# A fused attention and Mish layer on one core: packing the normalised output of four heads into dense 128-row tiles

## The chip, the cores and the metric

The kernel runs on one core of one Trainium2 chip. The time is the device time of one execution in microseconds (us). Five engines work side by side, each through its own instructions in order: PE (TensorE, matrix products), ACT (ScalarE, here above all exponentials), DVE (VectorE), POOL (GpSimd) and SP (SyncE, which here issues nearly all DMAs). A *profiled execution* is one execution taken by the hardware profiler; its *span* goes from the first to the last instruction.

## The reference

```python
def _A_ref(x, wqkv, wo):                      # x: 1 x 2048 x 640, bf16
    H = 32; Dh = 20
    q, k, v = (x @ wqkv) ...                  # each 32 heads x 2048 x 20
    p = softmax(q @ k.T * Dh ** -0.5)         # per head, 2048 x 2048
    return (p @ v) ... @ wo                   # heads side by side, then 640 x 640

def _B_ref(x, w1, b1, w2):                    # 640 -> 1536 -> 640
    h = x @ w1 + b1
    return (h * tanh(softplus(h))) @ w2       # Mish

g = sigmoid((x * gate_w).sum(-1))
return g * _A_ref(x, wqkv, wo) + (1 - g) * _B_ref(x, w1, b1, w2)
```

The bulk of the work is the softmax: 32 heads of 2048 x 2048 exponentials.

## The kernel before

**Heads and groups.** The 2048 query rows are cut into four chunks `c` of 512, the 32 heads into eight groups `g` of four heads. A head has only 20 channels, and the four heads of a group sit at steps of 32 rows of the 128 partitions, so that PE can work on four heads side by side in four strips of 32 rows. KT and QT hold keys and queries in this form. A *unit* is the score tile of one head for 128 keys and 512 queries; the kernel has 4 x 8 x 16 x 4 = 2048 of them. The work goes through groups (c, g): first chunks 0 and 1 in turn for each g, then chunk 2, then chunk 3, whose last group is cut into two halves of 256 queries (`CUTS`).

**Steps.** Three units make a *step* (`SLOT`), 683 in all. In each step PE computes three score tiles into PSUM (`score_mms`, line 1291), ACT exponentiates them (`emit_e`, line 1312) into ETS, and PE multiplies the exponentials of four heads by V (`pv`, line 1616), summing over the keys in one PSUM bank per group. A column of ones in V (row 0 of each head's 32 rows) gives the softmax's denominator. Two steps' scores are in PSUM at a time.

**Tiles given to DVE.** In many steps one of the three units goes to DVE instead (`choose`, `emit_x`, line 1358). DVE writes a scaled score as int16, whose bits read as fp16 are a rough exponential. Four such units make a *batch*; two shifted versions of it (`close`, line 1396, functions `below` and `above`) are added to the sum, so a batch is multiplied by V three times (named Y, U, E). A batch lives in buffers (pads) of 4 x 512 columns that are lent by other tensors while these are not in use: parts of PADS, W2R, REG, HB, KT, QT (`("q", n)`) and OTN (`("o", n)`). The follow-up instructions wait in queues (`soon`, of which there are `LANES`), out of which `work` fills DVE's time. The functions `patient` and `settle` may move some multiplications to POOL.

**The planner.** The order of every instruction on every engine is fixed ahead of the run, by a plan that is made in Python: `Plan.add` keeps an estimated time per engine, and the loop over the steps (lines 2002 to 2076) puts background tasks on PE where its estimate leaves room (`pick`, `put`), each with a due step. `choose` decides whether a step gives a unit to DVE, from DVE's estimated backlog, corrected by a hand-set list `NUDGE` (one value per eight steps), and from the tasks that are late (`room`, `behind`, `lag`). `fill_up` adds dummy products (`spin`, line 1983) where PE would stream less than the share `STREAM` or `SPUN` of a window of some 3.6 us.

**After a group.** `group_done` copies the sums out of PSUM to OUNG (line 1749), sends the denominators through a DMA to POOL (line 1767), which inverts them (line 1771), and through SUMS back to all rows (lines 1774 and 1780, four DMAs). Then one multiplication (`times`, line 1709) on DVE or POOL writes the normalised group to its place given by `otn`: OTN for chunks 0 and 1, QT for chunks 2 and 3. The place keeps the heads' steps of 32 rows: 80 of 128 rows hold data. The last groups of chunk 3 (from `DIRECT`) are inverted on DVE without DMAs.

**Output projection.** `p_task` multiplies one tile of 128 queries by one half (320 columns) of the output weights WOG, which lie in WOQ in the same form with zero rows in between (`load_wo`): a *half tile*, one product per group, eight in all, through `p_mm` and the helper `tall` (line 557). `tall` may issue a product as four of 32 rows. For chunk 3, `part_task` does the six groups that are done early and stores to PART; the last two groups (`late`) are added at the end (lines 2084 to 2110). `mix` (line 1124) applies the gate and adds the dense layer's part.

**Dense layer.** `load_w1` (line 976) brings w1 in pieces of 256 columns through two buffers, `h_task` computes h, `mish` the activation (line 1053 on ACT, 1077 and 1080 on DVE), `b_task` the product by w2. These run from some 210 us on, interleaved with the output projection.

**Queues.** SP issues its DMAs in the plan's order; each waits on SP for what it depends on. K and Q for groups 2 to 7 go through DRAM: packed products are stored (line 706, `shelve`) and fetched into the 32-row form (line 730, `fetch`). The packed K products are staged in OTN, in columns 6 and 7 of its eight (line 695).

Of the kernel before, what the change touches and what calls it, by code (L numbers as in the profile page):

```python
# [14 lines left out]
ALU = mybir.AluOpType  # L15
AX = mybir.AxisListType

P = 128
S = 2048
D = 640  # L20
NF = 1536
H = 32
DH = 20
NG = 8
# [15 lines left out]
OWE = -0.5  # L40
# [14 lines left out]
STREAM = 0.46  # L55
SPUN = 0.5
# [10 lines left out]
CALM_END = 20  # L67
# [3 lines left out]
LANES = 1  # L71
# [8 lines left out]
GIVE_BACK = 25  # L80
# [8 lines left out]
BEYOND = 0.4  # L89
SOONER = 3  # L90
# [11 lines left out]
PATIENCE = 5  # L102
# [4 lines left out]
EAGER = 65  # L107
LOAD = 0.85
MISH = 3.5
GROUP = 2.25  # L110
LAST = 0
END = 45
SHIFT = 0.4
LAG = 45
SPARE = 5
WINDOW = 3.6
# [14 lines left out]
PART_DUE = 15  # L131
LAST_DUE = 23
# [20 lines left out]
LEAD = 10  # L153
NUDGE = [1.5, -3.5, -4.2, -3.7, 0.8, 2.3, -2.2, 0, -5.3, 1.5, 0.7, 2.3, -1.5, 0, -3.7, -1.5, 6, 0.0, 2.3, 0, 0, -3.7, 0.8, -0.7, 1.5, 3.7, -3, 1.5, 0.8, 3.0, 1.5, 6, -0.7, -0.7, 5, 2.2, 0.0, 1.4, 2.2, 0.8, 1.5, 6, 0.0, 2.2, -0.7, 3.5, -3.0, 0.0, -3.7, -1.5, 0.6, -2.3, 1.5, -0.7, -0.7, 0.7, 5, -0.7, 0, 2.9, 0.7, 0.7, 6, 0, 0, 0.7, -0.7, -0.7, 5, -1.5, 1.5, 0.7, 1.5, -3.8, -2.2, -3.0, 1.5, 0, 6, -3.8, 1.5, 0.7, -3, 1.5, -3, 2.8, 6]
# [116 lines left out]
def bass_gated_mix__softmax_full_mha__dense_activation_mish__prompt_kernel(  # L271
# [97 lines left out]
    def pad_at(home):  # L369

        kind, n = home
        if kind == "p":
            return PADS[:, n, :].rearrange("p (a b t) -> p a b t", a=2, t=CW)
        if kind == "h":
            return HB[:, 1, 0:8, :].rearrange("p f t -> p (f t)").rearrange("p (a b t) -> p a b t", a=2, t=CW)
        if kind == "k":
            return KT[:, n, :].rearrange("p (a b t) -> p a b t", a=2, t=CW)
        if kind == "q":
            return QT[:, 2 * n:2 * n + 2, 0:2 * CW].rearrange("p a (b t) -> p a b t", t=CW)
        if kind == "o":  # L380
            return OTN[:, n // 2, n % 2 * 4:n % 2 * 4 + 4, :].rearrange("p (a b) t -> p a b t", a=2)
        return AREAS[n][1].rearrange("p (a b t) -> p a b t", a=2, t=CW)
# [37 lines left out]
    def attention(pl, fast):  # L420
# [178 lines left out]
        if fast:  # L599
# [102 lines left out]
            def shelve(k, name, c, rows, src, ev, n, i=0):  # L702
# [436 lines left out]
        late = every[len(early):]  # L1139
        last_t = [t for t in range(4) if not fast or t * P >= CUTS[-1][0]]  # L1140
# [15 lines left out]
        def p_task(c, t, half, due, rest=False):  # L1156

            tb = c * 4 + t
            some = late if rest else every
            needed = [g for g in some if g < NG - 1]  # L1160
            needed.append(next((k[1] for k, (at, w) in cut.items() if k[0] == c and at <= t * P < at + w), NG - 1))

            def ready():
# [4 lines left out]
                if fast and len(wog_ready) < 2 * HG + 1 or rest and (t, half) not in part_done:  # L1168
                    return None
                return [otn_done[(c, g)] for g in needed] + wog_ready  # L1170

            def finish(bank, last):
                otn_read[c % 2].append(last)
                if fast and c < 2 and len(otn_read[c]) == 8:
                    gained.extend(("o", 2 * c + i) for i in range(2))
                    pad_free.update({at: [last] for at in gained[-2:]})
# [21 lines left out]
        def part_task(t, half, due):  # L1198
# [14 lines left out]
            return Task([p_mm(c, t, half, g, early) for g in early], HALF * COL, finish, due, ready)  # L1213
# [33 lines left out]
        def emit_s(s):  # L1247
# [23 lines left out]
            if fast and order:  # L1271
                here = order[0][:2]
                for n in range(NG // 2):
# [4 lines left out]
                    if place[here] >= place[(2, 2 * n)]:  # L1278
                        given_back.add(at)
# [409 lines left out]
        spread_last = []  # L1689
        end_done = []  # L1690

        def group_done(c, g, step, last):
# [7 lines left out]

            def reads():
                if fast:
                    assert c != 2 or not pad_busy(("q", g // 2))
                    return [low_last[0], *lent(("q", g // 2), c == 2)] if c >= 2 else [zeros, *turned, *(k_moved if g >= 6 else ())]
                assert c < 2 or g > 0 or len(otn_read[c % 2]) == 8
                return otn_read[c % 2]

            def times(src, deps, eng="dve"):
                oung_free[0] = bc_read[0] = otn_done[(c, g)] = pl.add(eng, lambda e: e.tensor_tensor(
                    otn(c, g, fast), src, BC, ALU.mult), [*deps, *reads()], cost=WIDE if eng == "dve" else ASIDE, kind="L")  # L1710
                if g == NG - 1:
                    otn_read[c % 2] = []
# [543 lines left out]
```

## Time and profile before

| | |
|---|---|
| median of three runs | 767.94 us (767.77 to 768.16) |
| profiled execution, its own time | 767.94 us |
| its span | 766.1 us |
| first exponential tiles on ACT / last instruction | 9.06 us / 766.1 us |
| DMA traffic | 46.73 MB, mean 61 GB/s |

How to read the rows that follow in the prediction: a group row gives line, engine, operation, out<-in with the names of the program's tensors, the shape, the number of instructions (x), then `|` the busy time in us and the mean duration of one in ns, then `|` the engine's idle time just ahead of these instructions and what ended it. A row of the chain of waits gives start, length, engine, what was written, and line, in us. A row of the timeline gives start, length, engine, line, operation and shapes. Busy time is the union of an engine's instructions; a row that has a line number is a place in the kernel above.

### The profile page before, as it was taken

How to read it: one execution, taken by the hardware profiler on the slowest of the kernel's cores; microseconds unless marked ns; L12 is line 12 of the kernel's file. 1: busy time of each engine (PE TensorE's matmuls, PEld its weight loads, DVE VectorE, ACT ScalarE, POOL GpSimd, SP SyncE). 2: the span in 40 equal slices, each digit the busy share in tenths (PEclk: the TensorE clock that was granted, in tenths of full speed). 3: DMA queues.
4: the chain of work that ended last, by engine and by line, in shares of the span. 5: the costliest groups of instructions: out<-in, count | busy, mean ns of one | idle time of the engine just before them, and what ended most of it. 6: DMA issues, size and time to landing. Idle time of an engine off the chain costs nothing.

```text
span 766.1 us, 19028 instructions
## 1 busy us (share of the span) xinstructions
PE 731.2 (95%) x7922; PEld 272.4 (36%) x7922; DVE 697.0 (91%) x1325; ACT 751.1 (98%) x714; POOL 121.4 (16%) x60
## 2 busy tenths in 40 slices
PE   8999999899999999999999899999999999999996
PEld 4333334233333333222334433333333333433333
DVE  4789798899898999998999999999999999998895
ACT  6999999999999999999999999999999999999996
POOL 8111121011112021111011102121202111022000
PEclk9999999999999999999999999999999999999999
DMA  7411310221123312140113411022212213000001
GB/s 157 132 56 51 91 50 25 59 66 50 40 74 124 94 59 65 50 132 30 37 46 100 115 36 45 26 57 78 67 28 68 84 38 87 16 25 20 15 7 39
DMA packets 76586, 46.73 MB, mean 61 GB/s; under 512 B 23204, under 2 KB 72732, under 8 KB 76444
## 3 DMA queue, kind: packets, MB, share of 16 engines
q1 hardware_dynamic: 76380, 45.41, 21.3%
q8 instruction: 66, 1.08, 0.6%
q14 instruction: 28, 0.23, 0.1%
q0 software_dynamic: 112, 0.01, 0.1%
HBM read 35.74 MB, written 7.51 MB: 56 GB/s over the span
## 4 chain that ended last, share of the span: by engine, by line
ACT 83%; PE 15%; DVE 2%; issue 0%
ACT ETS L1312 80%; PE PS L1291 4%; PE PS L1616 4%; PE PS L557 3%; ACT REG L1053 2%; PE PS L1983 1%; ACT W2R L1053 0%; PE PS L635 0%; PE PS L936 0%; PE PS L829 0%; PE PS L866 0%; PE PS L764 0%; DVE WOQ L747 0%; DVE HB L2108 0%; PE PS L816 0%
## 5 line engine op out<-in xcount | busy, mean ns | idle before, releaser
L1312 ACT ACTIVATE ETS<-PS 128x1024 bf16<-128x1024 f32 (+1 forms) x683 | 731.1, 1279 | 3.1 <-PE PS L1291 2.3
L1291 PE MATMUL PS<-QT,KT 32*128 32x512 bf16 (+1 forms) x2112 | 270.8, 378 | 18.9 <-ACT ETS L1312 13.7
L1616 PE MATMUL PS<-ETS,V_all 128*21 128x512 bf16 (+1 forms) x1643 | 176.3, 375 | 0.0
L1771 POOL TENSOR_TENSOR RR<-RR,NEG 128x16 f32<-128x16 f32 x29 | 89.2, 3076 | 490.3 <-DMA RR<-OUNG 490.3
L1291 PEld LDWEIGHTS PS<-QT,KT 32*128 32x128 bf16 x2112 | 67.4, 91 | 231.0 <-ACT ETS L1312 179.7
L557 PE MATMUL PS<-XB,REG 128*32 128x256 bf16 (+3 forms) x716 | 82.1, 292 | 3.8 <-DVE HB L1030 1.6
L1358 DVE TENSOR_SCALAR QT<-PS 128x512 int16<-128x512 f32 x115 | 77.9, 686 | 6.4 <-PE PS L1291 5.8
L1358 DVE TENSOR_SCALAR PADS<-PS 128x512 int16<-128x512 f32 x106 | 71.7, 685 | 5.3 <-PE PS L1291 4.4
L557 PE MATMUL PS<-W2R,HB 128*128 128x320 bf16 (+1 forms) x600 | 73.0, 301 | 1.6 <-DVE XB L1102 0.6
L1358 DVE TENSOR_SCALAR OTN<-PS 128x512 int16<-128x512 f32 x79 | 53.7, 684 | 4.0 <-PE PS L1291 3.4
L557 PEld LDWEIGHTS PS<-XB,REG 128*128 128x128 bf16 (+1 forms) x716 | 38.1, 96 | 38.2 <-issue 28.9
L1616 PEld LDWEIGHTS PS<-ETS,V_all 128*21 128x21 bf16 x1643 | 41.3, 90 | 28.1 <-issue 23.1
L1080 DVE TENSOR_TENSOR U<-U 128x1024 f16<-128x1024 f16 x72 | 49.2, 683 | 0.2
L557 PEld LDWEIGHTS PS<-W2R,HB 128*128 128x128 bf16 (+1 forms) x600 | 33.2, 97 | 31.7 <-issue 16.0
L1358 DVE TENSOR_SCALAR REG<-PS 128x512 int16<-128x512 f32 x59 | 40.0, 687 | 3.7 <-PE PS L1291 3.2
L1030 DVE TENSOR_TENSOR HB<-PS,B1T 128x512 bf16<-128x512 f32 x48 | 32.8, 683 | 3.7 <-PE PS L557 3.3
L1358 DVE TENSOR_SCALAR KT<-PS 128x512 int16<-128x512 f32 x39 | 26.7, 686 | 5.7 <-PE PS L1291 5.6
L1077 DVE TENSOR_SCALAR U<-U 128x1024 f16<-128x1024 f16 x72 | 30.3, 420 | 0.5
L1396 DVE TENSOR_SCALAR QT<-QT 128x2048 int16<-128x2048 int16 (+2 forms) x62 | 29.2, 492 | 1.2 <-PE PS L1616 1.1
L557 PE MATMUL PS<-XB,WOQ 128*32 128x512 bf16 (+1 forms) x164 | 28.6, 382 | 0.8 <-DVE WOQ L775 0.4
L1358 DVE TENSOR_SCALAR W2R<-PS 128x512 int16<-128x512 f32 x35 | 23.7, 686 | 2.4 <-PE PS L1291 2.0
L557 PE MATMUL PS<-WOQ,QT 128*128 128x320 bf16 (+1 forms) x188 | 24.2, 301 | 1.6 <-DVE HB L1124 0.7
(173 smaller groups left out, 797.6 us busy)
## 6 DMA issues: line engine op xcount, KB each, us to landing
REG<-in_B_w_dram SPq DMA_DIRECT2D x36, 320.0 KB, 3.2
BCT<-SUMS SPq DMA_DIRECT2D x116, 64.0 KB, 2.1
W2R<-in_B_w_dram SPq DMA_DIRECT2D x12, 320.0 KB, 3.3
KT<-KS SPq DMA_DIRECT2D x28, 128.0 KB
QT<-QS SPq DMA_DIRECT2D x112, 20.0 KB
QS<-WOQ SPq DMA_DIRECT2D x16, 128.0 KB, 1.7
KS<-OTN SPq DMA_DIRECT2D x16, 128.0 KB, 1.7
W2R<-in_B_w_dram SPq DMA_DIRECT2D x1, 1920.0 KB, 8.2
```

The costliest lines, as they stand in the source:

```text
L557: op = e.matmul(PS[at, bank, cols], w[:, at], x, start=start, stop=stop, **({"tile_position": (0, i * rows)} if parts > 1 else {}))
L1030: ev = dve(lambda e: e.tensor_tensor(hb, PS[:, bank, :].rearrange("p (i t) -> p i t", i=2), bias, ALU.add), [last, b_load, *guarded, *b_re ...
L1053: ex = pl.add("act", lambda e: e.activation(U, h, AF.Tanh, scale=0.5, bias=-MISH_AT), [ev, u_free[0]], cost=0.95)
L1077: return lambda e: e.tensor_scalar(dst, src, *ops)
L1080: return lambda e: e.tensor_tensor(dst, one, two, ALU.mult)
L1291: op = pl.add("pe", lambda e, i=i, g=real(g), tile=tile, j=j, cols=cols, c=c, of_q=of_q: e.matmul(scores(s)[:, i, cols], KT[32 * j:32 * j ...
L1312: e_op[s] = pl.add("act", lambda e: e.activation(EXPS[:, at:at + n, :], scores(s)[:, 0:n, :], AF.Exp, scale=SCALE, bias=LIFT if fast else ...
L1358: ev = dve_by(lambda e: e.tensor_scalar(block(batch["y"], n, I16), scores(s)[:, 2, :], SCALE * ULPS, BIAS, ALU.mult, ALU.add), [s_op[s], * ...
L1396: op = pl.add("dve", lambda e, sp=sp: e.tensor_scalar(some_of(home, sp, I16), some_of(y, sp, I16), by, None, ALU.add), deps, cost=each, ki ...
L1616: lasts[n] = pl.add("pe", lambda e, v=v, j=j, src=src[:, cols], of_q=of_q, count=count: e.matmul(PS[32 * j:32 * j + EW, bank, of_q], v, sr ...
L1771: r = (pl.add("pool", lambda e: e.tensor_tensor(RR[:, :], RR[:, :], NEG[:, :].to_broadcast([P, 16]), ALU.pow), [got, m_neg], cost=INVERT) ...
L1983: pl.add("pe", lambda e: e.matmul(PS[:, bank, :], k[:, 0:P], k, start=True, stop=True), [free], cost=PASS, kind="S")
```

## The change

The normalised output of chunks 0 to 2, and of groups 0 to 5 of chunk 3, is no longer left in the 32-row form. `times` writes it to one of two staging places (column 5 of OTN's two halves); then DMAs on SP (`move`) copy each head's 20 rows, cut at multiples of 128, to dense tiles of 128 rows: channel `r` of the 640 goes to row `r % 128` of tile `r // 128`, five tiles per chunk, in OTN for chunks 0 and 1 and in QT for 2 and 3 (`packed`). The output weights are loaded dense as well (WOP, three DMAs), and in 32-row form for the last two groups alone (WOL, `spread_out`). A half tile then takes five products over 128 rows; `part_task` takes four (480 rows: three full tiles and one of 96); the late two groups remain as they were.

With it go three changes of buffers: OTN lends columns 0 to 3 of each half once its chunk is projected, and columns 6 and 7 of both halves once all K moves are done; QT's fourth pair is given back at group 4 of chunk 3 instead of group 6 of chunk 2. And the planner's numbers are changed: two lanes instead of one, other thresholds, and other values in `NUDGE` (87 values; their sum goes from 39.1 to 74.2, and over steps 576 to 639 it rises by 28.1).

```diff
-OWE = -0.5
+OWE = -0.1
...
-STREAM = 0.46
-SPUN = 0.5
+STREAM = 0.34
+SPUN = 0.4
...
-CALM_END = 20
+CALM_END = 60
...
-LANES = 1
+LANES = 2
...
-GIVE_BACK = 25
+GIVE_BACK = 50
...
-BEYOND = 0.4
-SOONER = 3
+BEYOND = 0.6
+SOONER = 8
...
-PATIENCE = 5
+PATIENCE = 3
...
-EAGER = 65
-LOAD = 0.85
-MISH = 3.5
-GROUP = 2.25
+EAGER = 90
+LOAD = 1.0
+MISH = 4
+GROUP = 2.5
...
-END = 45
-SHIFT = 0.4
-LAG = 45
-SPARE = 5
-WINDOW = 3.6
+END = 55
+SHIFT = 0.5
+LAG = 40
+SPARE = 3
+WINDOW = 4.0
...
-PART_DUE = 15
-LAST_DUE = 23
+PART_DUE = 18
+LAST_DUE = 13
...
-LEAD = 10
+LEAD = 16
...
         if kind == "o":
-            return OTN[:, n // 2, n % 2 * 4:n % 2 * 4 + 4, :].rearrange("p (a b) t -> p a b t", a=2)
+            return OTN[:, :, 6:8, :] if n == 2 else OTN[:, n, 0:4, :].rearrange("p (a b) t -> p a b t", a=2)
...
+    def packed(c, i):
+
+        return QT[:, i, (c - 2) * CW:(c - 1) * CW] if c >= 2 else OTN[:, c, i, :]
...
     WOG = WOQ[:, :].rearrange("p (g c) -> p g c", c=D)
+    WOP, WOL = WOG[:, 0:NFT, :], WOG[:, NFT:NFT + 2, :]
...
                 stage_free.setdefault((k, n), []).append(moved)
+                if k and len(k_moved) == 5 * NC:
+                    gained.append(("o", 2))
+                    pad_free[("o", 2)] = list(k_moved)
...
             def load_wo():
                 assert all(n in grams for n in range(3))
-                wo_v = A_wo.rearrange("(g j r) c -> j r g c", g=NG, j=HG, r=DH)
-                none = ZEROS.ap()
-                pieces = [(f"wo{j}", WOG[32 * j + 1:32 * j + 1 + DH, :, :], wo_v[j], 1.7) for j in range(HG)]
-                pieces.append(("wz", WOQ[0:P:32, :], none.to_broadcast([HG, NG * D]), 0.4))
-                pieces += [(f"wz{j}", WOQ[32 * j + 1 + DH:32 * j + 32, :], none.to_broadcast([32 - EW, NG * D]), 0.9)
-                           for j in range(HG)]
+                wo_p = A_wo.rearrange("(f p) c -> p f c", p=P)
+                pieces = [(f"wp{n}", WOP[:, a:b, :], wo_p[:, a:b, :], 1.5) for n, (a, b) in enumerate(((0, 2), (2, 4), (4, 5)))]
+                pieces += spread_out(WOL, NG - 2, 0.5)
...
         def p_mm(c, t, half, g, groups):
-            return tall(slice(0, HALF), otn(c, g, fast)[:, t * P:(t + 1) * P], WOG[:, g, half * HALF:(half + 1) * HALF],
+
+            rows = slice(0, P)
+            if g in groups and not isinstance(g, tuple):
+                x, w = otn(c, g, fast), WOL[:, g - NG + 2, :] if fast else WOG[:, g, :]
+            else:
+                x, w = packed(c, g[1]), WOP[:, g[1], :]
+                if g == groups[-1] and len(groups) < NFT:
+                    rows = slice(0, len(early) * HD % P)
+            return tall(slice(0, HALF), x[rows, t * P:(t + 1) * P], w[rows, half * HALF:(half + 1) * HALF],
                         g == groups[0], g == groups[-1])
...
+        def tiles_of(groups):
+
+            return [("t", i) for i in range(-(-len(groups) * HD // P))] if fast else list(groups)
...
-            some = late if rest else every
-            needed = [g for g in some if g < NG - 1]
+            some = late if rest else tiles_of(every)
+            needed = [g for g in (late if rest else every) if g < NG - 1]
...
-            return Task([p_mm(c, t, half, g, early) for g in early], HALF * COL, finish, due, ready)
+            some = tiles_of(early)
+            return Task([p_mm(c, t, half, g, some) for g in some], HALF * COL, finish, due, ready)
...
-                    if place[here] >= place[(2, 2 * n)]:
+                    if place[here] >= place[(2, 2 * n) if n < 3 else (NC - 1, 4)]:
                         given_back.add(at)
...
+            direct = not fast or c == NC - 1 and g in late
+
...
+            def move(src, op):
+
+                rows = sorted({*range(HD * g, HD * (g + 1) + 1, DH), *range(-(-HD * g // P) * P, HD * (g + 1), P)})
+                ops = []
+                for a, b in zip(rows, rows[1:]):
+                    i, j = a // P, (a - HD * g) // DH
+                    at = 32 * j + 1 + a - HD * g - DH * j
+                    deps = [op]
+                    if c < 2:
+                        deps += [zeros, *turned]
+                    else:
+                        assert not pad_busy(("q", i // 2))
+                        deps += [low_last[0], *lent(("q", i // 2))]
+                    ops.append(pl.add("sp", lambda e, a=a, b=b, i=i, at=at: e.dma_start(
+                        packed(c, i)[a - i * P:b - i * P, :], src[at:at + b - a, :]), deps, f"pk{moves[0] % 2}", cost=0.4))
+                return ops
+
             def times(src, deps, eng="dve"):
-                oung_free[0] = bc_read[0] = otn_done[(c, g)] = pl.add(eng, lambda e: e.tensor_tensor(
-                    otn(c, g, fast), src, BC, ALU.mult), [*deps, *reads()], cost=WIDE if eng == "dve" else ASIDE, kind="L")
-                if g == NG - 1:
+                to = otn(c, g, fast) if direct else OTN[:, moves[0] % 2, NFT, :]
+                op = oung_free[0] = bc_read[0] = otn_done[(c, g)] = pl.add(eng, lambda e: e.tensor_tensor(
+                    to, src, BC, ALU.mult), [*deps, *reads()], cost=WIDE if eng == "dve" else ASIDE, kind="L")
+                if not direct:
+                    staged[moves[0] % 2] = ops = move(to, op)
+                    moves[0] += 1
+                    otn_done[(c, g)] = ops[-1]
+                if g == NG - 1 and not fast:
                     otn_read[c % 2] = []
```

More of the change, by code (lines that the diff above doesn't have):

```diff
@@ L1167, in ready @@
                     return None
-                if fast and len(wog_ready) < 2 * HG + 1 or rest and (t, half) not in part_done:
+                if fast and len(wog_ready) < 2 * HG + 4 or rest and (t, half) not in part_done:
                     return None
@@ L1174, in finish @@
                 if fast and c < 2 and len(otn_read[c]) == 8:
-                    gained.extend(("o", 2 * c + i) for i in range(2))
-                    pad_free.update({at: [last] for at in gained[-2:]})
+                    gained.append(("o", c))
+                    pad_free[("o", c)] = [last]
                 add = PART[:, t, half, :] if rest else ball(tb, half)
@@ L1689, in attention @@
         spread_last = []
+        staged, moves = {}, [0]
         end_done = []
@@ L1699, in group_done @@
                     scale(after)
+            direct = not fast or c == NC - 1 and g in late
             def reads():
+                if fast and direct:
+                    assert not pad_busy(("q", g // 2))
+                    return [low_last[0], *lent(("q", g // 2))]
                 if fast:
-                    assert c != 2 or not pad_busy(("q", g // 2))
-                    return [low_last[0], *lent(("q", g // 2), c == 2)] if c >= 2 else [zeros, *turned, *(k_moved if g >= 6 else ())]
+                    return [*turned, *staged.get(moves[0] % 2, ())]
```

14 lines of the change are left out of this document (13 added, 1 removed).

## The prediction

> **What bounds the kernel now.** I read the page's busy table first, then the chain that ended last, then the groups by form, and then the windows.
>
> ```profile
> span 766.1 us, 19028 instructions
> PE 731.2 (95%) x7922; PEld 272.4 (36%) x7922; DVE 697.0 (91%) x1325; ACT 751.1 (98%) x714; POOL 121.4 (16%) x60
> ACT 83%; PE 15%; DVE 2%; issue 0%
> ```
>
> ACT is busy 98% of the span and carries 83% of the chain. The profiled execution took 767.94 us, which is also the median of the three runs, so 1.8 us lie around its span and a change of the span can be subtracted from 767.9 directly. The next view keeps the shapes of ACT's exponential (line 1312) apart.
>
> ```profile
> L1312 ACT ACTIVATE ETS<-PS 128x1024 bf16<-128x1024 f32 x457 | 463.8, 1136 | 1.7 <-PE PS L1291 1.1
> L1312 ACT ACTIVATE ETS<-PS 128x1536 bf16<-128x1536 f32 x226 | 345.1, 1568 | 1.4 <-PE PS L1291 1.3
> ```
>
> Each of the 683 steps makes three score tiles of 512 columns. Where the planner gave one of them to DVE, ACT exponentiates two (457 steps, 1136 ns), elsewhere three (226 steps, 1568 ns). **One more tile given away saves ACT 1568 - 1136 = 432 ns.** That is the only currency in which this kernel's time can fall by much: ACT waits for PE 1.7 + 1.4 us in all. What would buy it is time on DVE, so I cut the span into stages (columns: length, then busy time of PE, PEld, DVE, ACT, POOL).
>
> ```profile
> 30.00:120.00 90.00, 88.99 (x985) 33.12 (x977) 77.46 (x152) 90.00 (x87) 12.90 (x5) 1.00 0.21 62
> 120.00:215.00 95.00, 90.72 (x960) 31.95 (x957) 87.11 (x165) 94.18 (x92) 13.68 (x5) 1.00 0.16 47
> 215.00:255.00 40.00, 38.55 (x363) 12.66 (x361) 36.40 (x70) 39.78 (x39) 7.20 (x3) 1.00 0.36 107
> 255.00:350.00 95.00, 90.73 (x906) 29.95 (x905) 90.91 (x183) 94.31 (x93) 13.90 (x5) 1.00 0.27 78
> 350.00:450.00 100.00, 96.08 (x1074) 36.55 (x1072) 92.91 (x172) 100.00 (x95) 11.83 (x4) 1.00 0.23 63
> 450.00:570.00 120.00, 116.68 (x1285) 44.31 (x1283) 114.90 (x209) 120.00 (x116) 19.78 (x8) 1.00 0.17 48
> 570.00:640.00 70.00, 67.76 (x727) 27.07 (x724) 69.30 (x130) 69.85 (x67) 10.71 (x4) 1.00 0.24 66
> 640.00:757.00 117.00, 111.31 (x1325) 42.63 (x1324) 105.64 (x206) 117.00 (x111) 11.91 (x5) 1.00 0.07 20
> ```
>
> DVE's idle time is length less busy: 7.9, 3.6 and 4.1 us in the three stages from 120 to 350, 7.1 from 350 to 450, 5.1 from 450 to 570, 0.7 from 570 to 640, 11.4 from 640 to 757; together 39.9 us from 120 on. ACT is full in all of them.
>
> **The change part by part: the products.** The removed instructions are the output projection's, which read WOQ.
>
> ```profile
> L557 PE MATMUL PS<-WOQ,OTN x200: 299/299/310, 451.8 to 570.6; 128*128 128x320 bf16 x52, 128*32 128x320 bf16 x48
> L557 PE MATMUL PS<-WOQ,QT x188: 299/299/310, 643.6 to 761.6; 128*128 128x320 bf16 x108, 128*32 128x320 bf16 x80
> ```
>
> ```profile
> 486.59 0.31 PE L557 MATMUL PS<-WOQ,OTN 128*128 128x320 bf16 x1
> 493.33 0.72 PE L557 MATMUL PS<-WOQ,OTN 128*128 128x320 bf16 x4
> ```
>
> One product alone takes 0.31 us, four in a row 0.72, so a product costs (0.72 - 0.31) / 3 = 0.14 us of PE. Chunks 0 to 2 have 24 half tiles, which go from 8 products to 5: 72 fewer. The eight part tasks of chunk 3 go from 6 to 4 (three full tiles and one of 96 rows): 16 fewer. The two late groups of chunk 3 stay as they are. Together 88 x 0.14 = 12.3 us of PE: 48 products (6.7 us) between 452 and 571, and 40 (5.6 us) from 644 on. All of it lies beside ACT, which the chain of waits shows without a break there but for 12 us:
>
> ```profile
> 450.25 52.23 ACT ETS L1312 x50
> 607.55 1.35 ACT ETS L1312
> 619.91 9.27 ACT ETS L1312 x9
> 670.49 86.31 ACT ETS L1312 x81
> ```
>
> So the products alone are worth 0 us directly (only 607.55 to 619.91 runs through PE, and no output product is made there). What they can bring is indirect: a lighter PE makes score tiles in time for DVE. The view of line 1358, DVE's exponential, says that DVE stood idle ahead of it for this:
>
> ```profile
>   PE PS L1291: 26.6, 61
> ```
>
> **The price of one tile on DVE.** Successive 512-wide DVE instructions start 0.60 us apart, and a batch of four tiles needs two more instructions of 2048 columns (line 1396) of the same length:
>
> ```profile
> 242.13 0.68 DVE L1358 TENSOR_SCALAR W2R<-PS 128x512 int16<-128x512 f32 x1
> 242.73 0.68 DVE L1749 COPY OUNG<-PS 128x512 f32<-128x512 f32 x1
> 243.33 0.68 DVE L1358 TENSOR_SCALAR QT<-PS 128x512 int16<-128x512 f32 x1
> L1396 DVE TENSOR_SCALAR QT<-QT 128x2048 int16<-128x2048 int16 x25 | 17.2, 686 | 0.2 <-PE PS L1616 0.2
> ```
>
> That is 0.60 + 2 x 0.60 / 4 = 0.90 us of DVE for a tile. As the run gets 0.432 us shorter at the same time, closing one idle DVE microsecond buys 1 / (0.90 + 0.432) = 0.75 tiles, or 0.32 us. On PE the batch costs two further passes of four products:
>
> ```profile
> 492.46 0.39 PE L1616 MATMUL PS<-PADS,V_all 128*21 128x512 f16 x4
> 492.68 0.39 PE L1616 MATMUL PS<-ETS,V_all 128*21 128x512 bf16 x4
> ```
>
> Passes start 0.22 us apart, so a tile costs PE 0.11 us, and the 12.3 us freed would carry over a hundred tiles: from here DVE is the limit, not PE.
>
> **The planner's numbers, lanes and buffers.** The second queue for DVE's follow-up instructions, the later give-back of QT's fourth pair, the buffer in OTN's columns 6 and 7 that comes once the K moves are done, and the shifted thresholds issue nothing themselves; they decide how many tiles go to DVE. The corrections of DVE's backlog sum to 74.2 in place of 39.1, most of the rise (28.1) in steps 576 to 639. No row prices this. Bounds: below, tiles are lost (the slower rivals); above, all of the 39.9 us is filled. I take the idle time of the two stages that lose products, 5.1 + 11.4 = 16.5 us: that is where PE gets lighter. 16.5 x 0.75 = 12.4 tiles, x 0.432 = **5.3 us**.
>
> **The packing DMAs.** Per chunk the head boundaries and the boundaries at 128 rows make 4, 5, 4, 5, 5, 4, 5, 4 pieces: 36. Three chunks and six groups of the fourth (27) give 135 DMAs on SP's queue, each of 20 KB or less. The nearest rows are the query fetches of that size and two landings:
>
> ```profile
> L730 SPq DMA_DIRECT2D QT<-QS x112: 274/330/1298, 35.4 to 335.8; - x112
> KS<-OTN SPq DMA_DIRECT2D x16, 128.0 KB, 1.7
> REG<-in_B_w_dram SPq DMA_DIRECT2D x36, 320.0 KB, 3.2
> ```
>
> 135 x 0.33 = 45 us of SP over the whole run; each lands after 1.7 to 3.2 us, and I take 2. Nothing near waits for that: chunks 0 and 1 are projected from 452 us, chunk 2 from 644, tens of microseconds behind their last multiplication. Only chunk 3's sixth group is near its part tasks, and their 32 products (4.5 us) still have ACT's last 30 us as cover. If that cover goes, the cost is those 2 us. The loads of the output weights are smaller and end well ahead of 452: 0. The tail behind the last exponential has the same products as before: 0.
>
> The sum: 767.9 - 0 (products) - 5.3 (tiles) + 0 (DMAs) = **762.6 us**.
>
> **The rivals.**
>
> *All idle time closed.* Two lanes and one more buffer act from 120 us on, not only where products go. 39.9 x 0.75 = 30 tiles, 12.9 us: **755.0**. For it: DVE does reach 69.30 of 70 us in one stage. Against it: the 26.6 us of waits for scores are partly order, not load.
>
> *No more tiles.* The products were hidden, and 570 to 640 shows DVE full; if the number of tiles stays, the time stays at **767.9**. This is also the case in which the packing does what it says and nothing follows.
>
> *SP held up behind the multiplication: slower.* The packing DMAs wait on SP for the normalising multiplication (line 1709), and what stands behind them in SP's queue waits too: loads of w1 (line 976), stores, the next group's sums. Where the multiplication runs on POOL it has waited long for DVE's slots:
>
> ```profile
> L1709 POOL TENSOR_TENSOR QT<-OUNG,BCT x6: 1267/1272/1278, 469.0 to 707.4; 128x512 bf16<-128x512 f32 x6
> POOL OTN L1709 <- DVE KT L1396: 21.9, 2, 14.8
> POOL QT L1709 <- DVE OTN L1396: 17.8, 2, 9.2
> L976 SPq DMA_DIRECT2D REG<-in_B_w_dram x36: 367/390/1540, 299.9 to 642.5; - x36
> ```
>
> Those four waits average 9.9 us; with 1.3 for the multiplication and 5 x 0.33 for the issues SP is held some 13 us. The w1 loads stand (642.5 - 299.9) / 35 = 9.8 us apart and take 3.2 to land, with two buffers: a slack of 6.6 us. Beyond that the dense layer slips, by some 6 us for each of about five such groups: 30 us in which DVE lacks its Mish pieces. If none is refilled it costs 30 x 0.32 = 9.7 us, if all is, 0; half is 4.9: **772.8**. It decides where SP is held beyond 6.6 us with a w1 load behind. [...] The trace agrees that SP stands at such waits:
>
> ```profile
> SPq L976 <- PE PS L1616: 53.5, 19, 13.8
> ```
>
> *The clock: slower.* The changed thresholds (0.46 to 0.34, 0.5 to 0.4) let PE stream less before dummy products (line 1983) fill in, and real products go too.
>
> ```profile
> L1983 PE MATMUL PS<-KT 128*128 128x512 bf16 x53 | 16.1, 384 | 0.0
> busy tenths in 40 slices 0000000000000000062000000000000000000100
> L635 PE MATMUL PS<-ETS 128*128 128x512 bf16 x7 | 3.2, 630 | 1.2 <-DVE ETS L620 1.2
> 320.00:350.00 30.00, 29.06 (x259) 8.07 (x259) 28.00 (x56) 29.37 (x29) 5.05 (x2) 1.00 0.37 110
> ```
>
> The second line is the dummies' share of 40 slices of 19.2 us: nearly all stand from 326 to 364. The first products of the run take 630 ns, the same shape later 384. If half of the stage from 320 to 350 ran so, PE would need some 0.4 us more for each microsecond: 15 x 0.4 = 6 us, **774**. [...]
>
> **How the numbers follow.** Forecast 762.6 (759 to 766): 0.46. All idle time closed: 0.18. No more tiles: 0.14. SP held up: 0.17. Clock: 0.05. What a measurement tells from no change here is 0.2%, or 1.5 us. Faster is 0.46 + 0.18 = 0.64, the same 0.14, slower 0.17 + 0.05 = 0.22. The range goes from 754.5, just below the case with everything filled, to 770.0, which takes in a mild hold-up of SP; beyond it I leave the full hold-up and the clock, and a little below.
>
> **What would show each step.** Tiles: some 469 short and 214 long exponentials in place of 457 and 226, and DVE's idle time gone from 450 to 757; the same count would mean the second rival. Products: 168 by WOQ in place of 256 (a product that is issued in four parts of 32 rows counts four times in the rows). SP: a large wait of the new DMAs for the multiplication, with w1 products waiting for DMA. Clock: a window under 1.00, or score products over 384 ns. The forecast is wrong if the tile count moves by less than 5 or more than 20, or if ACT's waits for PE grow by some microseconds.

## The result and the profile after

The changed kernel takes 761.88 us (four runs, 760.74 to 763.08) beside 767.87 us for the kernel before; the ratio is 0.9922, with a 95% interval of 0.9904 to 0.9939. The forecast was 762.6 us, the range 754.5 to 770.0.

The page of the changed kernel opens like this:

```profile
span 759.4 us, 19104 instructions
PE 709.3 (93%) x7865; PEld 265.0 (35%) x7907; DVE 705.9 (93%) x1306; ACT 743.6 (98%) x714; POOL 123.2 (16%) x60
ACT 89%; PE 7%; DVE 2%; DMA 1%; issue 1%; SPq 0%; POOL 0%; POOLq 0%
```

ACT is still the bound and its share of the chain has grown. DVE has 8.9 us more work in a span that is 6.7 us shorter, so its idle time fell from 69.1 to 53.5 us. What it does with that time stands in the groups by form (ACT's exponential, now line 1345):

```profile
L1345 ACT ACTIVATE ETS<-PS 128x1024 bf16<-128x1024 f32 x475 | 483.5, 1140 | 2.0 <-PE PS L1324 1.5
L1345 ACT ACTIVATE ETS<-PS 128x1536 bf16<-128x1536 f32 x208 | 323.1, 1568 | 2.0 <-PE PS L1324 1.7
```

There are 475 short exponentials in place of 457: **18 more tiles go to DVE**, worth 18 x 0.432 = 7.8 us of ACT. (The last step has two tiles in any case, so a plan with n tiles shows n + 1 short exponentials.) ACT's idle time ahead of them rose from 3.1 to 4.0 us.

The rest of the span is its two ends. The timeline of ACT shows where the first exponentials start and the last ones end; first two rows of the kernel before, then two of the changed one (start, length in us):

```profile
9.06 5.48 ACT L1312 ACTIVATE ETS<-PS 128x1536 bf16<-128x1536 f32 x4 [1.05 <-PE PS L1291]
738.62 20.43 ACT L1312 ACTIVATE ETS<-PS 128x1536 bf16<-128x1536 f32 x17
```

```profile
9.52 5.62 ACT L1345 ACTIVATE ETS<-PS 128x1536 bf16<-128x1536 f32 x4 [1.05 <-PE PS L1324]
738.88 13.88 ACT L1345 ACTIVATE ETS<-PS 128x1024 bf16<-128x1024 f32 x11
```

Before, the last exponential ended at 738.62 + 20.43 = 759.05 and the tail behind it took 766.1 - 759.05 = 7.1 us; after, it ends at 752.76 and the tail takes 6.6. The account: -7.8 (tiles) + 0.9 (ACT waits) + 0.5 (a later first exponential) - 0.5 (tail) = -6.9, against -6.7 of the span. **The whole gain is tiles given to DVE.** The open question was what had made room for them: the five products, the buffers, or the planner's numbers.

The windows of the changed kernel (same columns as in the prediction) show where DVE's idle time went:

```profile
120.00:215.00 95.00, 89.70 (x959) 32.53 (x967) 87.66 (x159) 94.89 (x92) 12.84 (x5) 1.00 0.20 56
215.00:255.00 40.00, 37.41 (x366) 11.56 (x368) 39.01 (x72) 40.00 (x40) 6.12 (x2) 1.00 0.33 100
...
350.00:450.00 100.00, 95.39 (x1078) 37.17 (x1076) 96.38 (x177) 100.00 (x98) 16.84 (x7) 1.00 0.23 67
450.00:570.00 120.00, 114.62 (x1247) 43.64 (x1247) 118.04 (x224) 119.99 (x115) 20.29 (x8) 1.00 0.21 61
570.00:640.00 70.00, 63.46 (x742) 25.09 (x744) 68.34 (x131) 68.95 (x66) 10.73 (x3) 1.00 0.23 63
640.00:750.00 110.00, 101.98 (x1258) 36.26 (x1252) 106.53 (x196) 110.00 (x107) 10.61 (x4) 1.00 0.07 20
```

The last stage ends at 750 here, while the exponentials still run in both kernels. The kernel before has in it:

```profile
640.00:750.00 110.00, 105.25 (x1225) 39.70 (x1225) 102.06 (x199) 110.00 (x106) 11.91 (x5) 1.00 0.08 21
```

Idle on DVE is now 7.3, 1.0, 3.6, 2.0, 1.7 and 3.5 us in these stages; before it was 7.9, 3.6, 7.1, 5.1, 0.7 and 7.9. The two stages that lost output products, 450 to 570 and 640 to 750, gave 3.1 and 4.5 us. But the stage from 350 to 450, in which no output product runs in either kernel, gave 3.5 us too, and 215 to 255 gave 2.6. The view of DVE's own exponential by windows says how the tiles moved (length, busy, count), first before, then after:

```profile
350.00:450.00 100.00, 39.66 (x59) 1.00 0.23 63
450.00:570.00 120.00, 50.41 (x75) 1.00 0.17 48
...
640.00:750.00 110.00, 45.23 (x67) 1.00 0.08 21
```

```profile
350.00:450.00 100.00, 43.34 (x64) 1.00 0.23 67
450.00:570.00 120.00, 49.23 (x74) 1.00 0.21 61
...
640.00:750.00 110.00, 50.35 (x75) 1.00 0.07 20
```

From 450 to 570, where 48 products left PE, there is not one tile more. From 640 to 750 there are eight more. (The windows are cut by time, and the changed kernel is ahead by up to 6.7 us, some six steps, so counts by stage are good to a few tiles.)

### The profile page after: what moved, and what is told of

Read it like the earlier page. It is cut to its first block, busy times and chain, and to the rows that moved or that the text cites. A ratio compares the mean times of both kernels' runs of the same rounds, so it can differ in the third digit from the quotient of the medians.

```text
span 759.4 us, 19104 instructions
## 1 busy us (share of the span) xinstructions
PE 709.3 (93%) x7865; PEld 265.0 (35%) x7907; DVE 705.9 (93%) x1306; ACT 743.6 (98%) x714; POOL 123.2 (16%) x60
## 4 chain that ended last, share of the span: by engine, by line
ACT 89%; PE 7%; DVE 2%; DMA 1%; issue 1%; SPq 0%; POOL 0%; POOLq 0%
ACT ETS L1345 86%; PE PS L1324 2%; ACT REG L1058 2%; PE PS L1649 2%; PE PS L562 2%; ACT W2R L1058 1%; PE PS L2043 1%; DMA WOQ<-in_A_wqkv_dram 1%; DMA REG<-in_B_w_dram 0%; DVE QT L1391 0%; PE PS L837 0%; DVE U L1082 0%; PE PS L901 0%; DVE HB L2168 0%; DVE OTN L1429 0%
## 5 line engine op out<-in xcount | busy, mean ns | idle before, releaser
L1345 ACT ACTIVATE ETS<-PS 128x1024 bf16<-128x1024 f32 (+1 forms) x683 | 722.6, 1270 | 4.0 <-PE PS L1324 3.2
L1649 PE MATMUL PS<-ETS,V_all 128*21 128x512 bf16 (+1 forms) x1624 | 167.0, 375 | 0.5 <-ACT ETS L1345 0.5
L562 PE MATMUL PS<-XB,REG 128*128 128x256 bf16 (+3 forms) x703 | 78.5, 296 | 8.7 <-DVE HB L1035 2.6
L1391 DVE TENSOR_SCALAR OTN<-PS 128x512 int16<-128x512 f32 x112 | 76.0, 689 | 1.9 <-PE PS L1324 1.4
L562 PE MATMUL PS<-W2R,HB 128*32 128x320 bf16 (+1 forms) x666 | 73.8, 300 | 1.1 <-DVE OUTT L1148 0.5
L1391 DVE TENSOR_SCALAR PADS<-PS 128x512 int16<-128x512 f32 x90 | 61.2, 689 | 4.8 <-PE PS L1324 4.3
L562 PEld LDWEIGHTS PS<-W2R,HB 128*32 128x32 bf16 (+1 forms) x666 | 33.5, 97 | 31.5 <-issue 14.9
L1391 DVE TENSOR_SCALAR KT<-PS 128x512 int16<-128x512 f32 x51 | 34.5, 687 | 4.5 <-PE PS L1324 4.1
L1649 PE MATMUL PS<-QT,V_all 128*21 128x512 f16 x240 | 27.9, 384 | 0.0
L1429 DVE TENSOR_SCALAR OTN<-OTN 128x2048 int16<-128x2048 int16 (+2 forms) x42 | 25.8, 621 | 0.6 <-PE PS L1649 0.5
```

The lines of the kernel that those rows point to most:

```text
L562: op = e.matmul(PS[at, bank, cols], w[:, at], x, start=start, stop=stop, **({"tile_position": (0, i * rows)} if parts > 1 else {}))
L1345: e_op[s] = pl.add("act", lambda e: e.activation(EXPS[:, at:at + n, :], scores(s)[:, 0:n, :], AF.Exp, scale=SCALE, bias=LIFT if fast else ...
L1391: ev = dve_by(lambda e: e.tensor_scalar(block(batch["y"], n, I16), scores(s)[:, 2, :], SCALE * ULPS, BIAS, ALU.mult, ALU.add), [s_op[s], * ...
L1429: op = pl.add("dve", lambda e, sp=sp: e.tensor_scalar(some_of(home, sp, I16), some_of(y, sp, I16), by, None, ALU.add), deps, cost=each, ki ...
L1649: lasts[n] = pl.add("pe", lambda e, v=v, j=j, src=src[:, cols], of_q=of_q, count=count: e.matmul(PS[32 * j:32 * j + EW, bank, of_q], v, sr ...
```

## The experiments

Twelve kernels were run. Each is measured beside the kernel before on the same chip (767.8 to 768.1 us). *Tiles* are short exponentials less one, *ACT idle* is the idle time that the page gives for the exponentials, *tail* is the span less the end of the last exponential, from ACT's timeline.

| kernel | median us | ratio to before (95%) | tiles | ACT idle us | tail us |
|---|---|---|---|---|---|
| before | 767.87 | | 456 | 3.1 | 7.1 |
| changed | 761.88 | 0.9904 to 0.9939 | 474 | 4.0 | 6.6 |
| e1 old layout, new numbers | 775.45 | 1.0076 to 1.0110 | 465 | 6.2 | 15.1 |
| e2 new layout, old numbers | 775.77 | 1.0082 to 1.0116 | 461 | 10.4 | 6.8 |
| e3 changed, eight products, same plan | 770.69 | 1.0022 to 1.0047 | 474 | 9.7 | 6.6 |
| e4 changed, eight products planned | 769.11 | 0.9998 to 1.0018 | 471 | 4.2 | 13.5 |
| e5 changed, buffers as before | 768.89 | 1.0002 to 1.0022 | 458 | 3.5 | 6.9 |
| e7 changed, DMAs doubled, same plan | 784.11 | 1.0192 to 1.0226 | 474 | 26.6 | 6.8 |
| e8 before, five products, same plan | 768.73 | 0.9998 to 1.0017 | 456 | 3.2 | 6.8 |
| e9 old layout, refitted | 762.13 | 0.9901 to 0.9942 | 471 | 3.1 | 7.0 |
| e10 eight products, refitted | 766.10 | 0.9958 to 0.9989 | 470 | 6.1 | 7.0 |
| e11 changed, refitted | 760.98 | 0.9875 to 0.9920 | 478 | 5.7 | 6.7 |
| e12 changed, 45 DMAs, same plan | 761.80 | 0.9894 to 0.9942 | 474 | 4.1 | 6.6 |
| e13 true issue time, refitted | 765.72 | 0.9952 to 0.9974 | 468 | 5.7 | 6.6 |

### The two halves of the change alone

**e1** takes the kernel before and sets the 22 changed numbers (21 constants and the list `NUDGE`) to their new values.

```diff
-CALM_END = 20
+CALM_END = 60
...
-SOONER = 3
+SOONER = 8
...
-LAST_DUE = 23
+LAST_DUE = 13
```

> The kernel before with the changed planner's numbers alone (lanes, thresholds, backlog corrections); layout, buffers and eight products as before. Its plan gives 465 tiles to DVE (before 456, after 474). Theory A, only the number of tiles counts, at 0.432 us each: 767.9 - 9 x 0.432 = 764.0 us. Theory B, the numbers were fitted to the lighter PE and cost stalls or a longer tail in the old layout: no faster than 767.9. If the numbers alone were the whole gain: 761.9.

It took 775.45 us although it has nine tiles more. The exponentials do end as early as before, at 759.06, but then the chain of waits goes on for 15 us:

```profile
758.82 1.00 PE PS L557 x6
...
759.84 0.56 DVE W2R L1124
...
760.45 3.75 PE PS L557 x104
...
764.22 0.54 ACT PADS L1181
...
764.82 2.50 POOL HB L1184 x3
```

Products of the output projection (line 557) that the plan could not place ahead of the last exponential run behind it, one task after the other, through PE, DVE, ACT and POOL. So the tiles were there, and more was lost at the end: theory B.

**e2** is the changed kernel with the old numbers, the same edit the other way.

```diff
-CALM_END = 60
+CALM_END = 20
...
-SOONER = 8
+SOONER = 3
...
-LAST_DUE = 13
+LAST_DUE = 23
```

> The new layout, five products, packing DMAs and buffers, but all of the planner's numbers as before. Its plan gives 461 tiles. Theory A (tiles only): 767.9 - 5 x 0.432 = 765.7 us. Theory B, the lighter PE pays by itself: 762 or less. Theory C, the packing DMAs cost: 768 or more.

It took 775.77 us with 461 tiles. Its tail is short; ACT stalls instead, 10.4 us in all. The largest stall is at 254 us, where the chain shows a fetch of keys:

```profile
253.75 0.32 SPq L1834
...
254.11 3.93 DMA KT<-KS
...
258.18 0.61 PE PS L1324 x3
```

On SP the fetch stands behind the store of the inverted sums (line 1834), which waits for POOL (in the changed kernel such stores wait for POOL's inversion 27 times, 83.0 us in all). SP's timeline shows that POOL got its input late:

```profile
243.27 4.10 SPq L1759 DMA_DIRECT2D OTN<-OTN  x5
...
248.03 0.62 SPq L1827 DMA_DIRECT2D RR<-OUNG  x1
...
253.75 0.32 SPq L1834 DMA_DIRECT2D SUMS<-RR  x1
```

DVE had copied the sums out of PSUM by 242.77 (line 1809), but the DMA that takes the denominators to POOL (line 1827) left at 248.03, behind five packing DMAs (line 1759) and a load of w1. In the kernel before, at the same place, the copy ended at 243.41 and that DMA left at 243.44. So in this stall theory C holds: the packing DMAs cost, by way of what stands behind them on SP. The smaller stalls were not followed back. Neither half of the change is faster without the other; each costs about 8 us.

### Is PE's time free?

**e8** takes 88 products out of the kernel before and nothing else.

```diff
         def p_mm(c, t, half, g, groups):
+            if fast and len(groups) > 2 and g in ((2, 3, 4) if len(groups) == NG else (2, 3)):
+                none = lambda e, bank, parts=1: None
+                none.parts = HG
+                return none
```

> The kernel before with its plan untouched, but three of the eight products of each half tile (two of the six in a part task) are not issued, so three of the eight head groups are missing from the output of the projection. The same 88 products are gone from PE as in the change, with nothing else: no DMAs, no new buffers, 456 tiles. The prediction's step (0 us directly): 767.9, within 1.5 us. Rival, from the run with 88 more products in the changed kernel's plan, which cost 8.8 us: PE is scarce, and taking them away gives several us, below 765.

768.73 us, no gain. PE is lighter in the windows from 450 to 570 (first before, then e8) and ACT was full already:

```profile
450.00:570.00 120.00, 116.68 (x1285) 44.31 (x1283) 114.90 (x209) 120.00 (x116) 19.78 (x8) 1.00 0.17 48
```

```profile
450.00:570.00 120.00, 112.08 (x1194) 39.67 (x1191) 114.85 (x209) 120.00 (x116) 19.27 (x8) 1.00 0.17 48
```

**e3** goes the other way: it puts the 88 products back into the changed kernel behind the plan's back.

```diff
+            once = tall(*args, True, True)
+            def more(e, bank, parts=1):
+                for _ in range(3 if len(groups) == NFT else 2):
+                    once(e, bank, parts)
+                return fn(e, bank, parts)
```

> The changed kernel with the order of its plan untouched, but each half tile's first product is issued three more times (two more in a part task), so that PE does eight (six) again without the planner knowing: 88 more products of 0.14 us, 12.3 us of PE. Same 474 tiles. The prediction's step (products lie beside ACT, 0 us directly): 761.9, within 1.5 us. Rival (PE is scarce at that number of tiles): later by a good part of 12.3 us, 766 to 774.

770.69 us: 8.8 us for 12.3 us of PE. Tiles and tail are those of the changed kernel, but ACT's idle time is 9.7 us, 8.2 of it for score products, and the short exponentials' mean falls from 1140 to 1104 ns. They also overlap less: their lengths add up to 58 us more than their busy time in the changed kernel and to 47 us more in e3. **Taking 88 products away from PE in a fixed order was worth nothing here; adding as many cost seven tenths of their length.** In the one case ACT was already full, in the other the order had used the room.

**e4** lets the plan know of the eight products; the extra ones repeat the first product at the head of each task's list, three for a whole task and two for a part.

```diff
+XTRA = 3
...
-            return Task([p_mm(c, t, half, g, some) for g in some], HALF * COL, finish, due, ready)
+            return Task([p_mm(c, t, half, some[0], some[:1])] * (0 if rest or not fast else XTRA) + [p_mm(c, t, half, g, some) for g in some], HALF * COL, finish, due, ready)
```

> As the run before, but the three more products stand in the plan, so it makes room for them: 471 tiles. Theory A (tiles only): 761.9 + 3 x 0.432 = 763.2 us. Rival (PE is scarce): its plan is pushed into a longer tail or stalls, 766 or more.

769.11 us, by a long tail (13.5 us), as in e1 and as the rival had it; ACT idles 4.2 us. **e10** fits the corrections and the thresholds anew to this case (most of `NUDGE` and ten constants, three of them here).

```diff
-SOONER = 8
+SOONER = 6
...
-PART_DUE = 18
+PART_DUE = 21
-LAST_DUE = 13
+LAST_DUE = -3
```

> The changed kernel with eight products planned, as in the run before of that kind, and its numbers fitted anew to that: 470 tiles. If the 7 us that the planned products cost were a misfit of the numbers: 761.9 + 4 x 0.432 = 763.6 us or less. If they are PE's load: 766 or more.

766.10 us falls just inside the second answer, but the nine runs go from 764.03 to 767.88, so the time does not decide. The long tail is gone (7.0 us); that part had been a misfit. What is left against 763.6 goes with ACT's idle time of 6.1 us, and the chain shows one large part of it, a load of w1 that lands late (first fence). On SP it stands right behind four packing DMAs (second fence):

```profile
423.15 3.56 DMA REG<-in_B_w_dram
...
426.76 1.44 PE PS L563 x7
```

```profile
419.51 3.60 SPq L1760 DMA_DIRECT2D QT<-OTN  x4
423.15 0.48 SPq L985 DMA_DIRECT2D REG<-in_B_w_dram  x1
```

So what is left is not shown to be PE's load. ACT idles 2.29 us after this stall. How long the w1 load had been ready was not measured.

### Buffers and DMAs

**e5** drops the two gains of buffers.

```diff
-                if k and len(k_moved) == 5 * NC:
-                    gained.append(("o", 2))
-                    pad_free[("o", 2)] = list(k_moved)
...
-                    if place[here] >= place[(2, 2 * n) if n < 3 else (NC - 1, 4)]:
+                    if place[here] >= place[(2, 2 * n)]:
```

> The changed kernel without its two gains of buffers: OTN's columns 6 and 7 are not lent, and QT's fourth pair goes back when it did before. Five products, packing DMAs and the changed numbers stay. Its plan gives 458 tiles (16 fewer). Theory A (tiles at 0.432 us, no new stalls): 761.9 + 6.9 = 768.8 us. Rival (the lighter PE carries the gain and the buffers are incidental): below 765.

768.89 us, theory A to 0.1 us, with 458 tiles, ACT idle 3.5 us and a tail of 6.9. At these numbers, which were not refitted here, the new layout is worth nothing without the buffers.

**e7** issues a second DMA ahead of each packing DMA.

```diff
+                    def both(e, a=a, b=b, i=i, at=at):
+                        e.dma_start(SPARES.ap()[c * D + a:c * D + b, :], ZEROS.ap()[:, 0:CW].to_broadcast([b - a, CW])).then_inc(more_sem, 16)
+                        return e.dma_start(packed(c, i)[a - i * P:b - i * P, :], src[at:at + b - a, :])
```

> The changed kernel with the same plan, but ahead of each of the 135 packing DMAs SP issues a second DMA of the same size, from a row of zeros in DRAM to a place that nobody reads. It doubles SP's issue time for the packing (135 x 0.33 = 45 us more) without the plan knowing. The prediction's step (the packing DMAs cost 0): 761.9, within 1.5 us. Rival (SP's queue is held up, loads and fetches come late): ACT's stalls grow, 764 to 772.

784.11 us, 22 us more, far over what either theory gave. ACT waits for scores:

```profile
L1347 ACT ACTIVATE ETS<-PS 128x1024 bf16<-128x1024 f32 (+1 forms) x683 | 724.3, 1240 | 26.6 <-PE PS L1326 25.9
```

and the chain goes through SP (lines 1762 and 1763 are the added and the packing DMAs), for example

```profile
250.37 0.74 SPq L1763
251.15 0.68 SPq L1762
251.87 0.72 SPq L1763
...
255.11 4.02 DMA KT<-KS
```

Five packing DMAs and five added ones stand ahead of a key fetch. The transfers themselves are not slower: a w1 load takes 3.2 us from issue to landing, as in the changed kernel. It is the queue that is late. The issue time in these rows is 0.7 us, not the 0.33 us of the prediction. In the changed kernel, too (min/median/max in ns):

```profile
L1759 SPq DMA_DIRECT2D OTN<-OTN x72: 567/712/827, 58.5 to 394.9; - x72
L1759 SPq DMA_DIRECT2D QT<-OTN x63: 563/712/1347, 418.9 to 718.8; - x63
```

So the packing takes 135 x 0.712 = 96 us of SP, not 45. **e12** asks what that costs as the kernel stands; it cuts a group at multiples of 128 alone and keeps the plan's reckoning.

```diff
-                rows = sorted({...})
+                fine = sorted({...})
+                rows = [r for r in fine if r % P == 0 or r % HD == 0]
```

> The changed kernel with its plan untouched, but each group is packed by one or two DMAs (cut at multiples of 128 alone) in place of four or five: 45 in place of 135, with the same bytes. They take the group's rows as if they lay close together, so the packed channels are not the right ones. 90 issues fewer, which at the 0.7 us an issue that the traces show frees 63 us of SP. If the packing DMAs cost nothing as the kernel stands (the prediction's step): 761.9, within 1.5 us. If SP's queue costs already (the run with twice the DMAs was 22 us later): 756 to 760.

761.80 us: nothing, although the 45 DMAs take SP only some 26 us (medians of 0.586 and 0.556 us). So 70 us less on SP gave nothing, and 93 us more (135 x 0.689, in e7) cost 22 us.

**e13** puts the true issue time into the plan and fits the numbers again (most of `NUDGE` and six constants, two of them here).

```diff
-SOONER = 8
+SOONER = 11
...
-LAST_DUE = 13
+LAST_DUE = 40
...
-                        packed(c, i)[a - i * P:b - i * P, :], src[at:at + b - a, :]), deps, f"pk{moves[0] % 2}", cost=0.4))
+                        packed(c, i)[a - i * P:b - i * P, :], src[at:at + b - a, :]), deps, f"pk{moves[0] % 2}", cost=0.73))
```

> The changed kernel whose plan reckons 0.73 us for the issue of a packing DMA, as the traces show, in place of 0.4, with the numbers fitted anew to that: 468 tiles. Theory A (tiles alone): 761.9 + 6 x 0.432 = 764.5 us. If the wrong issue time costs the changed kernel stalls (w1 loads that come late), they are saved here: 762 or less.

765.72 us with ACT idle at 5.7 us: no stall was saved. At least with this fit, the true issue time in the plan gains nothing.

### Is the layout needed?

**e9** keeps the old layout, the old buffers and eight products, and fits the numbers anew, starting from the changed ones: values were varied, and those kept with which the plan came out shorter. Besides most of `NUDGE`, that moved five constants (shown against the changed kernel's values):

```diff
-LAST_DUE = 13
+LAST_DUE = -8
-PART_DUE = 18
+PART_DUE = 12
-SHIFT = 0.5
+SHIFT = 0.8
-SOONER = 8
+SOONER = 7
-CALM_END = 60
+CALM_END = 50
```

> The old layout, buffers and eight products with the changed numbers, but the backlog corrections and eleven thresholds fitted anew to this layout. Its plan gives 471 tiles (before 456, after 474) and has no long tail. Theory A (tiles, with stalls and tail as before): 767.9 - 15 x 0.432 = 761.4 us, so most of the gain is to be had without the layout. Theory B (at that many tiles the old layout's PE can't keep up): stalls grow by several us, 764 or more.

**762.13 us**, the changed kernel's time within either interval, with 471 tiles, ACT idle 3.1 us and a tail of 7.0:

```profile
L1312 ACT ACTIVATE ETS<-PS 128x1024 bf16<-128x1024 f32 x472 | 477.3, 1141 | 1.7 <-PE PS L1291 0.8 <-PE PS L1616 0.5
L1312 ACT ACTIVATE ETS<-PS 128x1536 bf16<-128x1536 f32 x211 | 324.8, 1567 | 1.5 <-PE PS L1291 1.2
```

**e11** fits the changed kernel further in the same way (most of `NUDGE` and seven constants, four of them here).

```diff
-BEYOND = 0.6
+BEYOND = 1.3
-SOONER = 8
+SOONER = 5
...
-PART_DUE = 18
+PART_DUE = 6
-LAST_DUE = 13
+LAST_DUE = 10
```

> The changed kernel with its numbers fitted further: 478 tiles. Theory A (tiles): 761.9 - 4 x 0.432 = 760.2 us. If DVE and PE have no more to give: 762 or more, with stalls in place of tiles.

760.98 us with 478 tiles: the fastest of all, though its interval (0.9875 to 0.9920) overlaps those of the changed kernel and of e9. In the profiled executions four more tiles, 1.7 us, are set against 1.7 us more of idle time on ACT.

## Why the prediction was right or wrong

**The bound and the currency: right.** Between the two kernels the number of tiles on DVE is what moved the time; in e1 to e4 and in e7, longer tails and ACT's waits outweighed it. e5 gives the price most cleanly: 16 tiles fewer were to cost 6.9 us by the 432 ns, and cost 7.0.

**Products worth 0 us directly: right, and shown** by e8. The same step's other half, that PE would hold over a hundred more tiles and DVE is the limit, did not hold: e3 showed that 12.3 us more on PE cost 8.8 us. Here PE's room could not be read from a sum over the span: 8.2 of the 9.7 us that ACT idled in e3 were waits for score products.

**12.4 tiles for 5.3 us: right in sign, mis-sized, and for the wrong reason.** There were 18 tiles. The idle time that DVE closed, 69.1 - 53.5 = 15.6 us, is close to the 16.5 us assumed, but only 7.6 of it (3.1 + 4.5) comes from the two stages that the prediction named. It also bought more: DVE's busy time rose by 8.9 us for 18 tiles, 0.49 us a tile, not 0.90. The rows of the tiles alone say something else. The first two fences are DVE's exponential (line 1358 before, 1391 after; busy and count over the whole span), the last two the shifted versions of a batch (line 1396 before, 1429 after):

```profile
0.00:766.10 766.10, 308.59 (x456) 1.00 0.22 61
```

```profile
0.00:759.40 759.40, 320.35 (x474) 1.00 0.23 65
```

```profile
0.00:766.10 766.10, 164.85 (x346) 1.00 0.22 61
```

```profile
0.00:759.40 759.40, 167.96 (x312) 1.00 0.23 65
```

The exponentials take 11.8 us more, 0.65 us each, no less than the 0.60 reckoned. The shifted versions take 3.1 us more in fewer instructions: 0.17 us a tile where 0.30 was reckoned. Together that is 14.9 us, and the engine's total rose by only 8.9. The total counts time in which neighbours overlap once (in the prediction's rows they start 0.60 us apart and last 0.68). So the mis-sized term is the room: a microsecond that length less busy calls idle took in more work than was reckoned. The place was half right. The prediction put the tiles where products left PE. From 640 to 750 there are eight more, but from 450 to 570 there is none, and from 350 to 450, where no product left, there are five. The lighter PE was not needed to let the tiles in: e9 reaches 471 tiles and 762.1 us with all eight products, by a fit of the planner's numbers alone. The prediction had taken the numbers as only deciding where the freed time goes. That the time came out within 0.7 us of the forecast is partly luck: 18 tiles are worth 7.8 us, of which waits, a later start and the tail took 0.9 back, and the median of the runs lies 0.6 us above the profiled execution (761.24).

**The packing DMAs at 0 us: right in cost** (e12), **wrong in size and in margin**: an issue takes 0.712 us, more than twice the 0.33 of the row that was taken for it (`QT<-QS`, 20 KB from DRAM to SBUF). What makes the difference stays open: e12's DMAs, also from SBUF to SBUF, took 0.56 to 0.59 us, and e7's added ones, from DRAM to DRAM, 0.69.

**Two lanes and a buffer in the rival "all idle time closed":** the buffers do matter (e5: 16 tiles at these numbers), but not all idle time closed; 120 to 215 still has 7.3 us. One lane alone was not tried on the chip.

**SP held up: not in the changed kernel as told, but it happens.** The packing DMAs did wait for the multiplication on POOL there, four times, 4.3 us on average where 9.9 was reckoned:

```profile
SPq L1759 <- POOL OTN L1765: 17.3, 4, 6.2
```

The one stall of the dense layer's products that the chain shows in the changed kernel has another cause (chain in the first fence, SP's timeline in the second):

```profile
579.16 3.44 DMA REG<-in_B_w_dram
```

```profile
578.78 0.33 SPq L1834 DMA_DIRECT2D SUMS<-RR  x1
579.16 1.00 SPq L984 DMA_DIRECT2D REG<-in_B_w_dram  x2
```

The w1 load stood behind the store of the inverted sums, not behind a packing DMA, and e12 has the same stall (3.47 us at 579.00) with 90 DMAs fewer. The rival's own order, with sums or a w1 load behind packing DMAs, shows in e2 and e10, and e7 shows what it can cost. In e2 the fetch of keys left SP at 254.11, 0.04 us behind the store of the inverted sums; in the changed kernel the w1 load left at 579.16, 0.05 us behind such a store, which itself began 0.02 us after POOL's inversion had ended (573.90 + 4.86 = 578.76).

**The clock: wrong as a rival here.** The granted clock in the changed kernel's profile is below 1.00 only in the tail (0.74 from 755 to 759.4 us, in which PE is busy for 0.65 us alone), and score products of 512 columns last 384 ns in both kernels. The price in this rival rests on the first products' 630 ns, and these fall from 1 to 4 us, where the granted clock reads 1.00 as well; no run here shows a slow clock at that price. Each of the two thresholds, set back alone, leaves the plan with the same tiles and the same planned length; neither was run on the chip.

**Still open** is what the layout is worth by itself. With numbers fitted to each, the new layout is 1.15 us ahead of the old one (e11 against e9), less than the intervals tell apart, and a longer fit might move either.

## What to carry to other kernels

Where a hand-made order runs at 98% of one engine, first ask which of the other engines can still take over some of that engine's work, and count that. Here, taking 88 products off another engine in a fixed order gave 0, and adding as many to another order cost 0.1 us a product. A structural change and the numbers that were refitted with it must be separated: here the old structure, refitted in the same way, was as fast. Price a DMA's issue by a row as like it as can be found, and look for what stands behind it in its queue.

## What was not expected of the hardware

- The issue of a packing DMA, 20 rows or fewer from SBUF to SBUF, held SP for 712 ns (median of 135), where a query fetch of 20 KB from DRAM to SBUF took 330 ns (median of 112).
- POOL's inversion of 128 x 16 values does not always take the same time. In POOL's timeline of the changed kernel it took 3.0 us at 550.74 and 4.86 us at 573.90, the one ahead of the late w1 load:

```profile
550.74 3.01 POOL L1831 TENSOR_TENSOR RR<-RR,NEG 128x16 f32<-128x16 f32 x1 [20.65 <-DMA RR<-OUNG]
...
573.90 4.86 POOL L1831 TENSOR_TENSOR RR<-RR,NEG 128x16 f32<-128x16 f32 x1 [11.16 <-DMA RR<-OUNG]
```

- The changed kernel's four runs spread over 2.3 us (760.74 to 763.08), the four of the kernel before beside them over 0.4 (767.77 to 768.16); no experiment tells why.
